# Two weight loads in two parts each over both DMA queues, a memset for padding zeros, a one-element first activation, and a list of tasks written anew

## The chip, the cores and the metric

The kernel runs on one core of a Trainium2 chip. The metric is the device time of one execution in microseconds (us); a kernel's time is the median of its runs. Before the change it is 303.88 us (three runs, 302.52 to 304.61). The engines are PE (TensorE, the matrix products; PEld are its weight loads), DVE (VectorE), ACT (ScalarE), POOL (GpSimd) and SP (SyncE, which here only issues DMAs). SP and ACT each issue DMAs on a queue of their own.

## The reference

A transformer block on x [2048, 640] in bf16: attention with a memory, then a dense layer with silu, both behind a layer norm and with a residual.

```
h  = x + attn(layernorm(x))        # 32 heads of 20, 4 segments of 512 tokens
    q, k, v = x @ wq, x @ wk, x @ wv
    per segment s:
        a_dot = softmax(q k^T / sqrt(20), causal) v
        a_mem = phi(q) M / (phi(q) z + 1e-6)
        o     = g * a_mem + (1 - g) * a_dot          # g = sigmoid(beta)
        M, z += phi(k)^T v, sum(phi(k))              # phi(t) = t + 1 or exp(t)
    attn = o @ wo
h2 = h + silu(layernorm(h) @ w1) @ w2                # 640 -> 1728 -> 640
```

## The kernel before

The work is cut into tasks (a load, a normalization of 128 tokens, a projection of one group of heads, a tile of scores, its exponentials, and so on), each with what it reads and writes. A list written out by hand, `ORDER`, gives the order in which the tasks are put on the engines; `/A`, `/D`, `/G`, `/S` after a name choose ACT, DVE, POOL or SP where a task can run on several, and numbers after a colon choose the buffers (PSUM banks, for instance). Each engine runs its own instructions strictly in the order of the list, and a tracker puts in the semaphore waits. So what stands before a task on its engine, and what it waits for, is all that sets its time.

Each of the four segments (512 tokens) goes through: layer norm and transposition of x (`n1_st` statistics, `n1_r` one over the root, `n1_ap` normalizing; then for segment 0 `n1_tp`, five products with the identity on PE, and `n1_te`, the copy of the transposed block to SBUF, and for the others a DMA transpose `n1_tr`); projections `pr` to q and k with their evacuation `qe`; values `v` with their evacuation `ve`; scores `qk` with their exponentials `e` on ACT, masks `mk` on POOL; products with the values `av`, evacuation `oe`, transposition back `tn` and normalizing `nm`; the memory `kt`, `mz`, `ma`, `mb`; the output projection `wo`; layer norm 2 (`n2_`); and the dense layer `h1`, `th`, `s`, `h2`, `o`, `out`. In segment 0 the tokens are taken in halves, x (the first 256) and y (the others). In a name like `pr020x` the digits are segment, group of heads, and 0 for q or 1 for k; in `e0x0` the group comes first.

The front, which the change touches most:

- SP and ACT issue the loads (lines 576 and 579): SP block 0 of x (`x0`), wq, three fifths of wv, blocks 4 to 7 of x, wo, beta, and then the parts of w1 and w2's last rows; ACT block 1 (`x1`), blocks 2 and 3 (`x2`), wk, the rest of wv.
- wq and wk come in the layout of the reference, 20 columns a head, and are rearranged for tiles of 32 rows a head: for each of five groups of heads a task `re_wq0` to `re_wq4` and `re_wk0` to `re_wk4`, of two or three copies each, on DVE (line 693) or ACT (line 691). Every one of them waits for the whole weight.
- `zpad` (line 592, DVE) zeroes a small tile. `warm` (line 594, ACT) is the first activation: it takes tanh of those zeros into the two last rows of w2's tile (128x1280), which the loads `w_w2_4` and `w_w2_5` then fill in part. The table of functions is loaded just ahead of it.
- `fill29` and `fill15` are products with zeros (line 613, 44 of them, 128x256) that feed nothing: PE runs them while it has no data.
- Block 1's and block 2's statistics run on ACT (lines 733 and 736), block 0's and block 3's on DVE (lines 741 and 744).
- `pr` products are at line 855, their evacuations at 863 (ACT) and 864 (DVE); scores at 932, their exponentials at 943.

## Time and profile before

| | us |
|---|---|
| median of three runs | 303.88 |
| the profiled execution | 303.13 |
| its span | 301.4 |
| first products with wq start | 10.43 |
| first scores start | 15.47 |
| first exponential starts | 15.86 |
| first evacuation of values starts | 27.40 |
| last product ends, about | 299.1 |

The span is the time from the first to the last instruction of one execution; some time lies around it. A row of the profile gives the start and the length of a group of instructions of one form; in brackets stand the idle time of the engine before it and what ended that. The rows of the stretches give how long each engine was busy in that stretch, the number of its instructions, the clock that PE was granted as a share of full speed, and the load of the DMA engines.

### The profile page before, as it was taken

To read this page: it belongs to the slowest core of one execution; us is meant where nothing else is said; L and a number is where in the kernel's file an instruction comes from. 1 tells how busy PE (TensorE), PEld (TensorE's weight loads), DVE (VectorE), ACT (ScalarE), POOL (GpSimd) and SP (SyncE) were. 2 spreads that over 40 slices of the span, in tenths; PEclk is the share of its full clock that TensorE was granted. 3 is DMA by queue.
4 is the path that set the end of the run, shared out by engine and by line. 5 is a ranking of instruction groups with operands and counts; after the bars stand their busy time and mean duration, and the time that the engine had idled before them with its cause. 6 is when DMAs were issued, how large, how long until landed. Compare 5 with 4: busy or idle time off the path is not lost.

```text
span 301.4 us, 7509 instructions
## 1 busy us (share of the span) xinstructions
PE 289.2 (96%) x2995; PEld 172.9 (57%) x3017; DVE 222.7 (74%) x516; ACT 226.0 (75%) x322; POOL 141.0 (47%) x267
## 2 busy tenths in 40 slices
PE   8799789999999999999999999999999999999996
PEld 6576445455655655656644544466565457764575
DVE  3879977977649789989679885868956786844613
ACT  6799998999999999999589889986778841004500
POOL 6678933344627555745647247574763430200000
PEclk9799999999999999999999999999999999999999
DMA  7998524405454301261741300234220013321001
GB/s 254 362 370 125 96 56 118 107 17 157 79 108 90 59 19 21 40 97 22 110 126 42 81 4 20 39 70 73 66 65 24 0 24 65 67 65 46 0 30 59
DMA packets 48723, 24.66 MB, mean 82 GB/s; under 512 B 39153, under 2 KB 47601, under 8 KB 48689
## 3 DMA queue, kind: packets, MB, share of 16 engines
q1 hardware_dynamic: 45116, 19.92, 29.4%
q10 hardware_dynamic: 3572, 4.27, 4.9%
q8 instruction: 24, 0.39, 0.5%
q14 instruction: 11, 0.08, 0.1%
HBM read 10.41 MB, written 2.62 MB: 43 GB/s over the span
## 4 chain that ended last, share of the span: by engine, by line
PE 68%; DVE 15%; ACT 10%; POOL 3%; issue 2%; ACTq 1%; DVEq 0%; POOLq 0%
PE ps_all L1235 18%; PE ps_all L1193 15%; PE ps_all L855 9%; ACT PT L943 7%; PE ps_all L1158 6%; PE ps_all L932 5%; PE ps_all L820 5%; PE ps_all L975 4%; DVE stt L741 3%; PE ps_all L1004 2%; PE ps_all L1008 1%; POOL PT L954 1%; DVE oTs L990 1%; PE ps_all L1097 1%; DVE on L1041 1%
## 5 line engine op out<-in xcount | busy, mean ns | idle before, releaser
L943 ACT ACTIVATE PT<-ps_all 128x1024 bf16<-128x1024 f32 (+1 forms) x168 | 156.6, 988 | 16.8 <-PE ps_all L932 16.1
L954 POOL TENSOR_SCALAR_AFFINE_SELECT PT<-PT 128x512 bf16<-128x512 bf16 x128 | 82.1, 645 | 68.7 <-ACT PT L943 66.1
L1235 PE MATMUL ps_all<-w_sb,sT 128*128 128x320 bf16 (+2 forms) x462 | 64.8, 295 | 0.1
L1193 PE MATMUL ps_all<-hT,w_sb 128*128 128x512 bf16 (+1 forms) x315 | 60.4, 335 | 1.1 <-issue 0.6
L1202 ACT ACTIVATE th<-ps_all 128x512 f32<-128x512 f32 (+2 forms) x70 | 34.7, 510 | 34.4 <-PE ps_all L1193 26.9
L1235 PEld LDWEIGHTS ps_all<-w_sb,sT 128*128 128x128 bf16 x462 | 43.2, 98 | 18.6 <-issue 2.4
L1208 DVE SCALAR_TENSOR_TENSOR sT<-th,ps_all 128x512 bf16<-128x512 f32 (+2 forms) x70 | 38.0, 558 | 12.7 <-ACT th L1202 11.9
L1193 PEld LDWEIGHTS ps_all<-hT,w_sb 128*128 128x128 bf16 x325 | 30.0, 98 | 24.0 <-issue 2.3
L1248 DVE SCALAR_TENSOR_TENSOR x_tok<-ps_all,x_tok 128x640 bf16<-128x640 f32 (+3 forms) x18 | 13.4, 748 | 22.3 <-PE ps_all L1235 22.1
L762 POOL TENSOR_TENSOR rst<-rst,eps_c 128x1 f32<-128x1 f32 x32 | 18.3, 574 | 23.3 <-DVE rst L756 21.2
L741 DVE BATCH_NORM_STATS2 stt<-x_tok 128x6 f32<-128x320 bf16 x60 | 26.3, 479 | 2.1 <-DMA x_tok<-in_A_x_dram 1.7
L1049 POOL TENSOR_TENSOR otok<-on 128x320 bf16<-128x320 bf16 x24 | 19.4, 811 | 14.7 <-DVE on L1041 14.7
L1158 PE MATMUL ps_all<-wo_sb,oT 128*128 128x320 bf16 x160 | 24.3, 299 | 0.5 <-DVE Vx L831 0.5
L975 PE MATMUL ps_all<-PT,Vx 128*32 128x256 bf16 (+3 forms) x576 | 23.1, 287 | 1.1 <-DVE rd L1021 0.7
L864 DVE CAST QK<-ps_all 128x512 bf16<-128x512 f32 x24 | 16.4, 684 | 5.4 <-PE ps_all L855 5.2
L1041 DVE TENSOR_TENSOR on<-ps_all,rd 128x640 bf16<-128x640 f32 x24 | 19.8, 824 | 0.8
L1158 PEld LDWEIGHTS ps_all<-wo_sb,oT 128*128 128x128 bf16 x160 | 14.8, 98 | 8.0 <-issue 2.7
L990 DVE TENSOR_SCALAR oTs<-ps_all,lsc 128x256 bf16<-128x256 f32 (+1 forms) x30 | 17.8, 610 | 1.3 <-PE ps_all L975 1.0
L820 PE MATMUL ps_all<-wv_sb,xT 128*128 128x320 bf16 x120 | 18.3, 299 | 0.4 <-DVE otok L1023 0.3
L975 PEld LDWEIGHTS ps_all<-PT,Vx 128*32 128x32 bf16 x576 | 12.2, 96 | 11.0 <-issue 3.2
L768 DVE TENSOR_SCALAR xn_rot<-x_tok,mvt,rst 128x640 bf16<-128x640 bf16 x32 | 14.8, 468 | 4.8 <-POOL rst L762 4.8
L855 PE MATMUL ps_all<-xT,wkr 128*128 128x512 bf16 x70 | 17.6, 380 | 0.5 <-issue 0.3
(88 smaller groups left out, 353.6 us busy)
## 6 DMA issues: line engine op xcount, KB each, us to landing
w_sb<-in_B_w_dram SPq DMA_DIRECT2D x5, 432.0 KB, 11.9
x_tok<-in_A_x_dram SPq DMA_DIRECT2D x3, 640.0 KB, 11.2
out_dram<-x_tok SPq DMA_DIRECT2D x9, 160.0 KB, 1.8
w_sb<-in_B_w_dram SPq DMA_DIRECT2D x2, 480.0 KB, 4.3
out_dram<-x_tok ACTq DMA_DIRECT2D x6, 160.0 KB, 2.0
sT<-in_A_wq_dram SPq DMA_DIRECT2D x1, 800.0 KB, 6.5
sT<-in_A_wk_dram ACTq DMA_DIRECT2D x1, 800.0 KB, 10.2
wo_sb<-in_A_wo_dram SPq DMA_DIRECT2D x1, 800.0 KB, 13.2
```

The costliest lines, as they stand in the source:

```text
L741: T.add(DV, lambda e, hh=hh: e.bn_stats(out=stt[:, s, 6 * hh:6 * hh + 6], in_=xb[:, 320 * hh:320 * hh + 320]), reads=R((xa, xsub)), writes ...
L820: fns.append(lambda e, c=c, hh=hh: e.matmul(bank(ps, hh)[:, 0:320], lhsT=xT_[:, c, 128 * i:128 * i + 128], rhs=wv_sb[:, c, 320 * hh:320 * ...
L855: fns = [lambda e, kc=kc: e.matmul(bank(ps)[:, lo:hi], lhsT=wt[:, kc, c, :], rhs=xT_[:, kc, lo:hi], start=(kc == 0), stop=(kc == NC - 1)) ...
L943: T.add(AC, lambda e: e.activation(out=pt[:, pta.slot, q0:q0 + 2, 0:width], in_=sc3[:, b0:b0 + 2, 0:width], func=ACT.Exp, scale=SCALE), re ...
L954: T.add(PO, lambda e: e.affine_select(out=v, in_=v, pattern=[[0, 4], [1, 128]], compare_op=ALU.is_ge, fill=0.0, base=0, channel_multiplier ...
L975: fns.append(lambda e, j=j, r=r, h=h, pa=pa, pt=pt, co=co, q0=q0, ji=ji: e.matmul(bank(po)[32 * r:32 * r + 32, q0:hi], lhsT=Vx[:, vx.slot, ...
L1041: T.add(DV, lambda e: e.tensor_tensor(out=on[:, ona.slot, :, :].rearrange("p b (x e) -> p b x e", e=DH), in0=v[:, :, :, 0:DH], in1=r2.unsq ...
L1158: fns.append(lambda e, c=c, hh=hh: e.matmul(bank(ps, hh)[:, 0:320], lhsT=oT[:, c, 128 * i:128 * i + 128], rhs=wo_sb[:, c, 320 * hh:320 * h ...
L1193: fns = [lambda e, c=c: e.matmul(bank(ps)[:, lo:hi], lhsT=w1_sb[:, c, 128 * f:128 * f + 128], rhs=hT[:, c, lo:hi], start=(c == 0), stop=(c ...
L1202: T.add(AC, lambda e: e.activation(out=th[:, tha.slot, lo:hi], in_=bank(ps)[:, lo:hi], func=ACT.Tanh, scale=0.5), reads=R((ps, [0])), writ ...
L1208: T.add(DV, lambda e: e.scalar_tensor_tensor(out=sT[:, f, lo:hi], in0=th[:, tha.slot, lo:hi], scalar=1.0, in1=bank(ps)[:, lo:hi], op0=ALU. ...
L1235: fns.append(lambda e, f=f, t0=t0, fr=fr, hh=hh, n=n: e.matmul(bank(pa, hh)[:, 0:n], lhsT=sT[:, f, t0:t0 + 128], rhs=w2_sb[:, fr, c0 + 320 ...
```

## The change

- wq and wk are each loaded in two parts, rows 0 to 383 on SP's queue and rows 384 to 639 on ACT's. The rearranging tasks wait for both parts.
- w2's padding zeros come from a memset (`w2z`, DVE), and `warm` writes a single element per partition to a tile of its own, `wj`.
- The list is written anew, with other engines for some tasks: in the front, ACT takes one block's statistics (block 0) instead of two, and three rearranging tasks (`re_wq1`, `re_wq4`, `re_wk0`) instead of one (`re_wq4`); there are 38 fillers in three tasks instead of 44 in two. Later, ACT takes `oe1x` and `ma00`; `ve21` goes to DVE; of the loads of w2's main parts, `w_w2_0` and `w_w2_1` go from ACT's queue to SP's and `w_w2_2` from SP's to ACT's; `vt16` (a copy of the heads that lie across tiles) goes from ACT's queue to SP's. PE's products keep nearly their order; at the end the last outputs are ordered otherwise.

```diff
@@ ORDER (first rows, and single rows of the rest)
-x1:3 mt0:0 epsc halfc mta0 mt1 epsg0 mt2 iota mta1 mtb1 x0:7 w_q:0 mm5 x2:5,0 w_k w_wv0:0 x4:1,2,4,6 w_wo:0 beta mta2
-mtb2 mt3 mta3 w_wv1 zpad sel warm:0 w_w2_4 w_w1_2:0 x8/S:8,9,10,11 w_w1_1 n1_st0/D:1,0 mm10 n1_st1/A:6 w_w1_0 w_w1_4
-n1_r0/G n1_ap0:0 mtb0 w_w2_5 mm6 mtb3 n1_r1/D n1_st3/D:0 w_w1_3 n1_r3/G n1_st2/A:2 n1_ap1:1 re_wq0/D:0 re_wq1/D
-n1_r2/G n1_ap3:2 mm11 re_wq2/D mm8 n1_ap2:3 re_wq3/D mm1 mm7 mm4 mm0 re_wk0/D:0 re_wk1/D fill29:0 fill15:1 re_wk2/D
-re_wk3/D n1_st6:5 n1_tp0:3 n1_te0/A:0 vpad1 mm9 vpad0 mm3 n1_tp1:0 n1_r6/G n1_te1/A mm2 re_wq4/A pr020x:2 n1_tp2:3
-n1_te2/A qe020x/A:0 pr000x:0 n1_tp3:6 n1_te3/A pr010x:1 qe010x/A:0 qe000x/A:0 pr001x:3 qe001x/A pr011x:4 qe011x/A
-qk0x0:0 e0x2:0 pr001y:5 e0x0 pr021x:6 qe001y/D qe021x/A n1_st4:7 n1_r4/G pha001:2 re_wk4/D pr040y:7 qe040y/A:0 ex001:1
+x1:3 mt1:0 mt0 halfc x0:7 w_q1:0 x2:5,0 mta0 mtb0 mm2 mm9 w_q0 w_k0 mt3 w_wv0:0 x4:1,2,4,6 iota w_wo:0 beta w2z/D:0
+zpad w_w2_4 w_w1_2:0 w_w1_4 w_w2_5 epsc sel mta3 vpad1 w_k1 w_wv1 x8/S:8,9,10,11 warm n1_st0/A:1,0 vpad0 mtb3 mm8
+n1_st1/D:6 n1_r1/D n1_ap1:1 mta1 w_w1_1 re_wq1/A:0 re_wq0/D n1_r0/G n1_ap0:0 re_wq2/D epsg0 n1_st3/D:0 mtb1 mm3 mt2
+mta2 mm11 mm1 n1_r3/G mtb2 n1_st2/D:2 n1_r2/D n1_ap3:2 re_wk1/D:0 n1_ap2:3 w_w1_0 w_w1_3 re_wk4/D re_wk3/D re_wq3/D
+fill6:0 fill27:1 fill5:2 mm7 mm6 mm4 mm5 mm10 mm0 n1_tp1:0 n1_te1/A:0 re_wk2/D n1_tp0:4 n1_te0/A pr020x:7 pr000x:2
+pr010x:0 re_wq4/A n1_tp3:3 re_wk0/A pr001x:5 qe000x/A:0 qe010x/A:0 qe020x/A:0 n1_te3/A qe001x/A n1_tp2:0 n1_te2/A
+pr011x:2 qk0x0:3 pr040y:7 pr001y:0 qe011x/D e0x0:0 e0x2 mk0x_0 qe001y/D qe040y/A:0 qk1x0:1 e1x0:1 pha001:2 mk0x_256
...
-nm4x:0 pha011:2 av1x:7 mk0yb_256 e7x2:2 oe1x/D:0 e7x0 mk7x_0 ve02/A phb011 n1_r8/G n1_ap8:3 qk5x0:0 v11:4 mk7x_256
+qk6x0:1 mk5x_256 oe1x/A:0 e6x2:1 e6x0 mk6x_0 mk6x_256 pha011:2 phb011 tn2x:7 av7x:0 nm2x:1 mk0yb_256 oe7x/D:1 tn1x:7
...
-ma13 oe11/A:0 ve20/D:0 n2_ap2:2 n2_tr2 e12e0:0 e12e2 mk12e_0 mk13a_0 mk12e_256 phb111 v21:0 ve21/A mz12:7 ma12 mz10:2
+e13b0:1 ma10 e13b2 mk12e_0 mk13b_0 mk13b_384 ve21/D mk12e_256 pr210:2 qe210/D:0 ex210:0 pr231:3 qk14a0:4 qe231/D:0
...
-o15_1 out15_1/A h2_13_0:4 h2_12_0:0 h2_12_1 h2_12_2 h2_12_3 o12 out12/S h2_15_1_0 h2_13_1 h2_13_2 h2_13_3 o13 out13/A
-h2_15_2_0 h2_15_3_0 o15_0 h2_15_0_2:6 h2_15_1_2 out15_0/A h2_15_2_2 h2_15_3_2 o15_2 out15_2/S
+h2_12_2 h2_12_3 o12 out12/S h2_15_2_0 h2_15_3_0 o15_0 out15_0/S h2_15_2_2 h2_15_3_2 o15_2 out15_2/A
@@ build
+    wj = sb("wj", [128, 1], F32)
...
-    load_w("q", wraw[:, 0, :, :], cw(A_wq), -99, 6.58, [(sT0, ["q"])], "fix", (SP,))
-    load_w("k", wraw[:, 1, :, :], cw(A_wk), -99, 8.51, [(sT0, ["k"])], "fix", (AC,))
+    for wi, (k, A_w) in enumerate((("q", A_wq), ("k", A_wk))):
+        load_w(k + "0", wraw[:, wi, 0:3, :], cw(A_w[0:384, :]), -99, 4.0, [(sT0, [k + "0"])], "fix", (SP,))
+        load_w(k + "1", wraw[:, wi, 3:5, :], cw(A_w[384:640, :]), -99, 2.7, [(sT0, [k + "1"])], "fix", (AC,))
...
-    G.task("warm", {AC: 1.15}, lambda e_: T.add(AC, lambda e: e.activation(
-        out=w2_sb[:, NF - 1:NF + 1, :], in_=zpad[:, 0:1].unsqueeze(2).to_broadcast([128, 2, D]), func=ACT.Tanh),
-        reads=R((C, ["zpad"])), writes=R((W["w2"], [4, 5]))), [(C, ["zpad"])], [(W["w2"], [4, 5])], -100)
+    G.task("warm", {AC: 0.2}, lambda e_: T.add(AC, lambda e: e.activation(
+        out=wj[:, :], in_=zpad[:, 0:1], func=ACT.Tanh), reads=R((C, ["zpad"])), writes=R((C, ["wj"]))),
+        [(C, ["zpad"])], [(C, ["wj"])], -100)
+    G.task("w2z", {PO: 1.3, DV: 0.4}, lambda eng: T.add(eng, lambda e: e.memset(w2_sb[:, NF - 1:NF + 1, :], 0.0),
+           writes=R((W["w2"], [4, 5]))), [], [(W["w2"], [4, 5])], -100)
...
-            rr, ww = [(sT0, ["qk"[wi]])], [(W[k], [c])]
+            rr, ww = [(sT0, ["qk"[wi] + "0", "qk"[wi] + "1"])], [(W[k], [c])]
```

The numbers in a task's declaration (4.0, 1.3, 0.4 and the like) are a planner's costs; they change nothing in the instructions.

More of the change, by code (lines that the diff above doesn't have):

```diff
@@ new lines @@
+nm1x:3 av3x:4 oe3x/D:0 ve11/A:1 qk0ya0:0 e0ya2:5 tn7x:7 nm7x:2 tn3x:4 nm3x:1 mz00:5 ma00/A:0 mb00:0 av5x:6 oe5x/D:0
+av6x:7 e0ya0 oe6x/D:1 qk1ya0:2 e1ya2:0 tn5x:6 nm5x:3 tn6x:7 nm6x:0 ot1:0 ot0 v10:0 ve10/D kt01:1 e1ya0 qk2ya0:4
+e2ya0:2 av0y:2 v12:0 oe0y/D:1 e2ya2 qk2yb0:2 w_w2_0/S e2yb0:1 e2yb2 mk2yb_0 mk2yb_256 ve12/D wo1:6 rs1 qk3ya0:0 wo0:4
+n2_st1:5 tn0y:7 nm0y:1 rs0 n2_r1/G n2_ap1:3 e3ya0:3 e3ya2 n2_st0:3 n2_r0/D n2_ap0:1 av1y:6 oe1y/A:0 qk4ya0:0 e4ya2:4
+pr101:7 v13:5 ve13/D e4ya0 qk3yb0:0 n2_tr1:0 qe101/A:0 pha101:2 n2_tr0 e3yb0:5 e3yb2 mk3yb_0 pr120:4 av2y:7 ex101:2
@@ new lines @@
+e16e0:5 e16e2 mk16e_0 pr230:4 qe230/D vt211/S vt27/S pha230:0 mk16e_256 vt22/S v22:6 vt25/S vt24/S ve22/D pha240:0
+pha231:0 phb231 ex220:0 qk17b0:2 ex240:2 phb240 vt28/S e17b0:3 vt21/A vt210/S h1_0_13_1:0 th0_13_1:1 s0_13_1 e17b2
+mk17b_0 h1_0_11_1:1 wo6:6 rs6 th0_11_1:0 ex230:1 qk18b0:2 e18b0:0 s0_11_1 mk17b_384 e18b2 mk18b_0 av16:0 oe16/D:1
+wo7:6 phb230 rs7 n2_st7:4 n2_r7/G qk17a0:0 e17a2:6 mk18b_384 e17a0 mk17a_0 wo4:4 rs4 n2_st6:6 ex241:2 h1_0_3_1:7
+th0_3_1:0 n2_r6/G h1_0_9_1:6 th0_9_1:1 qk18e0:0 wo5:4 e18e0:1 e18e2 s0_3_1 s0_9_1 n2_ap7:0 rs5 n2_ap6:2 mk18e_0
```

173 lines of the change are left out of this document (82 added, 91 removed).

## The prediction, made before the changed kernel was run

> **What bounds the kernel now.** I read the page first, then busy time in stretches, then the engines' timelines of the first 28 us, then the DMA issues.
>
> ```profile
> span 301.4 us, 7509 instructions
> ...
> PE 289.2 (96%) x2995; PEld 172.9 (57%) x3017; DVE 222.7 (74%) x516; ACT 226.0 (75%) x322; POOL 141.0 (47%) x267
> ```
>
> PE is busy for all but 12.2 us. By stretches (time, PE, PEld, DVE, ACT, POOL, then the granted clock):
>
> ```profile
> 0.00:10.00 10.00, 7.12 (x54) 5.58 (x54) 4.60 (x17) 7.00 (x13) 6.53 (x30) 1.00 0.84 281
> 10.00:20.00 10.00, 9.57 (x87) 7.60 (x88) 7.88 (x31) 7.87 (x20) 5.89 (x22) 0.83 1.06 365
> 20.00:30.00 10.00, 9.86 (x103) 6.88 (x101) 9.83 (x34) 9.93 (x19) 9.10 (x23) 1.00 0.90 192
> 30.00:40.00 10.00, 8.08 (x143) 4.40 (x140) 9.63 (x30) 9.12 (x14) 9.19 (x17) 1.00 0.41 74
> 60.00:80.00 20.00, 19.30 (x249) 11.91 (x248) 15.39 (x42) 19.87 (x32) 8.86 (x15) 1.00 0.36 91
> ```
>
> From 20 us on nothing waits long for anything: PE, DVE and ACT are full together, and later PE and ACT. So time won at the front is kept only if all three get it. The front is the one stretch with slack, and it runs like this (start, length, engine):
>
> ```profile
> 1.11 6.38 PE L613 MATMUL ps_all<-zpad 128*128 128x256 bf16 x44 [1.11 <-DVE zpad L592]
> ...
> 2.92 1.28 ACT L594 ACT_TABLE_LOAD   x1 [2.92 <-issue]
> ...
> 4.21 1.27 ACT L594 ACTIVATE w_sb<-zpad 128x1280 bf16<-128x1280 bf16 x1
> ...
> 10.43 0.85 PE L855 MATMUL ps_all<-hT,wqr 128*128 128x256 bf16 x5 [1.23 <-DVE wqr L693]
> ...
> 11.96 2.46 DVE L693 COPY wkr<-sT 128x400 bf16<-128x400 bf16 x9 [0.44 <-DMA sT<-in_A_wk_dram]
> ...
> 15.47 0.34 PE L932 MATMUL ps_all<-w_sb 20*128 20x256 bf16 x8
> ```
>
> The first products start at 10.43, the rearranging of wk waits for its load at 11.96, the first scores (qk0x) start at 15.47, their exponentials (e0x) at 15.86. The loads (KB, us from issue to landing):
>
> ```profile
> sT<-in_A_wq_dram SPq DMA_DIRECT2D x1, 800.0 KB, 6.5
> sT<-in_A_wk_dram ACTq DMA_DIRECT2D x1, 800.0 KB, 10.2
> ...
> x_tok<-in_A_x_dram ACTq DMA_DIRECT2D x1, 320.0 KB, 5.4
> ```
>
> **The loads.** With their issue times 1.25, 1.73 and 1.23 (and 2.33 with 11.4 to landing for wv's second part) the queues deliver: SP 160 KB (block 0 of x) by 3.79, 960 KB (and wq) by 7.75, 1440 KB (and half of wv) by 10.52, 2080 KB by 13.58; ACT 160 KB by 3.98, 480 KB by 6.63, 1280 KB (and wk) by 11.93, 1600 KB by 13.73. I interpolate on these. After the change SP carries x0 160, wq 480, wk 480; ACT x1 160, wq 320, x2-3 320, wk 320. The wq parts end at 640 KB on SP, 6.17, and 480 KB on ACT, 6.63: wq is there 1.1 us earlier. x2-3 end at 800 KB on ACT: 8.75 instead of 6.63, 2.1 later. The wk parts end at 1120 KB on both: 8.67 and 10.87, so wk is 1.1 earlier. wv's second part lands near 12.8, far ahead of its use at 25.7; x4 to x7 are some 0.7 later, behind 160 KB more.
>
> Equal shares of the two queues, half each of what both have brought by then (1609 KB at 7.75, 324 KB a us after it), would put x2-3 at 7.7 and wk at 9.7. But at 11.93 ACT's queue has brought 1280 KB and SP's some 1735, so I stay with the rows. The rule of equal turns is that of the Trainium skill, DMA: Bandwidth & Descriptors (Queues, rings and completion order: each DMA engine goes round robin over the queues by packets).
>
> **ACT's first work.** One more issue (0.57, as wk's row) puts the 1.28 table load at 3.49 to 4.77. The 1.27 activation shrinks to about 0.2 (the 128x32 exp takes 0.22): done at 4.99 instead of 5.48. ACT then does one block's statistics, 1.77 as in 5.39 to 7.16: 6.76. The second block that it had goes to DVE.
>
> **The zeros.** A DVE memset 128x640 in 32-bit words, ahead of zpad's. zpad's 128 took 0.17, so between 0.17 and five times that, 0.83; I take 0.7. It delays the fillers from 1.11 to 1.8, which PE has to spare: block 1 of x lands at 3.98, and statistics (1.10), rstd (0.15 and 0.56) and the normalizing (0.45) with hops of about 0.1 bring it to PE at 6.4. By the instruction order all 38 fillers (44 before) stand in one run ahead of the first transpose: none comes between products. Five products of the same 256 columns start to start take 1.07 at the half clock and 0.54 at the full, so 0.213 and 0.109 each; 44 in 6.38 us then turn fast at 4.0 (an estimate), and 38 from 1.8 end at 7.0, before ACT is free for the first copy of hT (7.6). If that cover is gone it costs up to 0.6.
>
> **The front, step by step.** POOL and DVE need 0.81 from the end of ACT's statistics to block 0's rstd (7.16 to 7.97) and 0.12 and 0.45 to apply it: 8.15. Transposes on PE 0.45, copy on ACT 0.70: 9.35. With 0.1 more the first products start at 9.45, 1.0 earlier; three of them at 0.54 end at 11.05. DVE meanwhile: wq's piece 8.55, x2-3 landed 8.75, two statistics of 0.89+0.21 to 10.95, rstd 0.15, apply 11.55, a piece of wk 11.9, apply 12.35. PE's transposes of blocks 3 and 2 follow at 11.6 and 12.55. ACT, in its order: wq's last piece 0.92 to 10.3; a piece of wk, waiting for 10.87, to 11.65; three evacuations (0.94) to 12.6; block 3's hT 13.25; the k evacuation 13.6, which opens the first scores at 13.65, 1.8 earlier; block 2's hT; e0x at 14.3, 1.55 earlier. ACT is the last to arrive.
>
> **The clock.** PE fell to half in the front:
>
> ```profile
> 10.00:11.00 1.00, 0.57 (x5) 0.93 1.07 362
> 11.00:12.00 1.00, 1.00 (x9) 0.50 1.07 364
> ```
>
> It lasts to 14.2, and products in it take 1.07 instead of 0.54. From 7.5 to 10.9 PE was busy for 1.19 of 3.4 us; after the change it has about 2.0, so I take full clock. With the fall it costs: the scores come at 14.6, e0x at 14.75, a loss of 0.45 of the gain. TensorE: Matmul & The Clock Gate in the Trainium skill (Part 1) has the clock drop after an idle window of about 3.4 us; the window here wasn't idle, so the trace shows the drop at a 35% busy share, and its bound remains open.
>
> **Up to 45 us.** ACT took 11.54 from e0x0 (15.86) to the first value evacuation (27.40) almost without a gap. The new list puts one more projection evacuation there (0.30): 26.15, a gain of 1.25. DVE ends its weight pieces at 14.25, about as before (14.34), but four pieces rather than one have come forward, with re_wk4's 0.50 done, and it hands oe1x (0.48) to ACT: 1.1 gained by 40 us. PE's 1.8 covers both. I take 1.2. ACT gets oe1x (0.47) and ma00 (about 0.3), which lie in its 0.88 of waits for PE at 36 to 39 us; without that cover they cost 0.77.
>
> **After 45 us.** The list shifts PE's work by few places. Off ACT go one of two w2 issues (0.38), a virtual-head issue (0.7) and ve21 (0.71): 1.8 us where ACT is over 94% full. The gain lies between nothing (DVE pays 0.83 for ve21; PE's idle is the ceiling, and from 60 to 140 it is 2.1 in all) and 1.8; I take 0.4, as most of PE's idle time is also in DVE's hands. The first w2 load now goes over SP's queue ahead of the two hT transposes; issued at 45.7 with 4.0 to landing it is done at 49.7, before the first of them at 50.7. Moving wk's and wq's issues on SP delays wo and beta by one issue, 0.5: both are used much later. At the tail the last product group is the same 128 columns, and o12 (0.82) now stands right before the last two outputs on DVE: -0.1.
>
> **Sum.** 1.2 + 0.4 - 0.1 = 1.5. The profiled execution took 303.13 (span 301.4 and 1.73 around it), so 301.6; it lies 0.75 under the median of the runs, 303.88, from which I get 302.4. One per cent, 3.0 us, is about what a measurement can tell.
>
> **Rivals.**
> - *More is kept* (300.6). If the queues do share equally, wk at 9.7 lets ACT go on at 10.3, and e0x comes at 13.7: 0.55 more. With ACT's relief worth 1.8 instead of 0.4, the gain is 3.3. For it: ACT at 19.87 of 20. Against: the shares above.
> - *Nothing arrives* (303.9). x2-3 are 2.1 later, and DVE, which now does both blocks' statistics, starts them then. If they land at 10 rather than 8.75, block 2's hT and DVE's remaining pieces slip by 1.25, and the 1.2 is gone.
> - *ACT becomes the bound of the first segment* (304.5, slower). If wk lands at 11.93 as before, e0x comes at 15.35 and ACT's lead of 0.5, less 0.3 for the extra evacuation, is 0.2; oe1x and ma00 then find no waits of ACT to hide in, 0.77, and the tail takes 0.1: 0.65 slower. It decides from about 11.4 on. For it: ACT is 9.93 of 10 busy there. Against: its waits at 36 to 39.
> - *It doesn't do what it says*: that holds for the fillers, which aren't between products. If the clock falls in spite of the earlier products, 0.45 is lost: 302.8, inside the forecast.
>
> **How the numbers follow.** Forecast 302.4: 0.52, own range 301.4 to 303.3. More kept: 0.16. Nothing: 0.15. ACT bound: 0.17. The range 300.6 to 304.6 takes in the three rivals at their prices and leaves out their far halves, 0.2 in all. Faster by over 1% (under 300.84): most of the second case, 0.14. Slower by over 1% (over 306.9) needs more than the third case prices, a stage of the redone list that fits worse on the chip: 0.06. Within: 0.80.
>
> **What would show it.** Right: wq's first piece before 7.2, first products near 9.5, first scores near 13.7, e0x near 14.3, the first value evacuation near 26.1, and ACT's share above 60 us a little lower. Wrong: wk's first piece later than 11.4; a granted clock of 0.5 after 9.5; DVE waiting for x2-3 beyond 9.5; or a front that is earlier and a stretch from 30 to 60 us with more PE idle time than its 2.65 us.

## The result and the profile after

The changed kernel takes 305.06 us (median of 20 runs, 303.47 to 306.57) and the kernel before, beside it, 303.38 (20 runs, 302.50 to 306.16). The ratio is 1.0042, with a 95% interval of 1.0023 to 1.0062: 1.3 us slower, where the prediction had 1.5 us faster. The profiled execution took 305.88, 0.8 more than the median; its span is 304.1.

The page of the profile after; before, the span was 301.4 us and PE was busy for 289.2:

```profile
span 304.1 us, 7512 instructions
...
PE 289.5 (95%) x2989; PEld 171.4 (56%) x3011; DVE 222.4 (73%) x506; ACT 225.4 (74%) x326; POOL 141.8 (47%) x273
```

The rows of the engines for the front of the changed kernel (start, length, engine; in brackets the idle time before and what ended it):

```profile
9.36 1.81 PE L859 MATMUL ps_all<-hT,wqr 128*128 128x256 bf16 x15 [0.80 <-ACT hT L790]
...
10.78 0.83 ACT L695 ACTIVATE wkr<-sT 128x400 bf16<-128x400 bf16 x2 [0.67 <-DMA sT<-in_A_wk_dram]
...
13.47 0.34 PE L936 MATMUL ps_all<-w_sb 20*128 20x256 bf16 x8
...
25.92 0.74 ACT L834 ACTIVATE Vx<-ps_all 128x640 bf16<-128x640 f32 x1
```

The first products (10.43 before) start 1.1 earlier, the first scores (15.47) 2.0 earlier, and the first evacuation of values (27.40) 1.5 earlier. The front did what it was meant to. By stretches (time, PE, PEld, DVE, ACT, POOL, granted clock, load of the DMA engines, GB/s) the changed kernel then shows:

```profile
20.00:30.00 10.00, 9.25 (x101) 5.68 (x99) 9.79 (x31) 9.18 (x18) 9.34 (x28) 1.00 0.87 194
30.00:40.00 10.00, 7.71 (x101) 4.03 (x101) 7.57 (x23) 7.25 (x12) 6.09 (x11) 0.83 0.34 72
60.00:80.00 20.00, 19.50 (x245) 11.24 (x246) 15.29 (x42) 19.86 (x31) 7.99 (x13) 1.00 0.39 99
120.00:140.00 20.00, 18.66 (x220) 11.42 (x219) 18.17 (x41) 17.82 (x27) 10.80 (x17) 1.00 0.32 62
```

Two stretches are new. Between 30 and 40 all three full engines have gaps (DVE 7.57 against 9.63, ACT 7.25 against 9.12), and the clock is 0.83. Between 120 and 140 PE is busy for 18.66 instead of 19.26, as the kernel before has it:

```profile
120.00:140.00 20.00, 19.26 (x226) 11.78 (x224) 18.64 (x42) 18.96 (x31) 13.04 (x23) 1.00 0.40 63
```

Here is the first of the two in the changed kernel, in PE's rows:

```profile
30.44 0.25 PE L1012 MATMUL ps_all<-ident,oTs 128*128 128x84 bf16 x2
32.10 0.51 PE L936 MATMUL ps_all<-w_sb 20*128 20x256 bf16 x8 [1.41 <-DVE rd L1025]
32.54 2.82 PE L824 MATMUL ps_all<-wv_sb,hT 128*128 128x320 bf16 x10
```

The row at 32.10 is `qk7x0`, the first scores of heads that lie across tiles. Their queries and keys come by twelve small copies `vt0…`, issued on SP's and ACT's queues. The bracket names a DVE instruction; the weight load of the same line shows what came last. From the waits of PE's weight loads (in all, times, longest), and SP's queue:

```profile
PEld ps_all L936 <- DMA w_sb<-w_sb: 1.5, 1, 1.5
```

```profile
22.00 7.42 SPq L899 DMA_DIRECT2D w_sb<-w_sb  x8
```

SP issues its eight copies in one unbroken run from 22.00 to 29.42. Before, the run was from 23.16 to 29.52:

```profile
23.16 6.36 SPq L895 DMA_DIRECT2D w_sb<-w_sb  x8
```

The last copy lands at 32.01 in this trace and at 32.27 in that of before, where `qk7x0` started at 32.33: there too it started as the last copy had landed, only that PE was busy until then. So the copies land 0.3 earlier, and `qk7x0` starts at 32.10, though the scores ahead of it are 1.3 to 3.1 earlier. While PE waits, its clock falls to half, and the ten products `v02` behind it take 2.82 instead of 1.5. The lead is gone and 0.9 us are lost when this execution comes to `qk2yb0` at 46 us. From there to the end of the products its lag grows from 0.9 to 2.6 us.

### The profile page after: what moved, and what is told of

Read it like the earlier page. It is cut to its first block, busy times and chain, and to the rows that moved or that the text cites. A ratio compares the mean times of both kernels' runs of the same rounds, so it can differ in the third digit from the quotient of the medians.

```text
span 304.1 us, 7512 instructions
## 1 busy us (share of the span) xinstructions
PE 289.5 (95%) x2989; PEld 171.4 (56%) x3011; DVE 222.4 (73%) x506; ACT 225.4 (74%) x326; POOL 141.8 (47%) x273
## 4 chain that ended last, share of the span: by engine, by line
PE 73%; DVE 11%; ACT 9%; DMA 3%; issue 2%; ACTq 1%; DVEq 0%
PE ps_all L1239 20%; PE ps_all L1197 16%; PE ps_all L859 9%; PE ps_all L824 7%; PE ps_all L936 6%; PE ps_all L1162 6%; ACT PT L947 6%; PE ps_all L979 4%; DMA sT<-in_A_wk_dram 3%; PE ps_all L1008 2%; PE ps_all L1101 2%; PE ps_all L1012 1%; DVE on L1045 1%; DVE sT L1212 1%; DVE x_tok L1170 1%
## 5 line engine op out<-in xcount | busy, mean ns | idle before, releaser
L1206 ACT ACTIVATE th<-ps_all 128x512 f32<-128x512 f32 (+2 forms) x70 | 34.6, 510 | 34.2 <-PE ps_all L1191 19.6
L745 DVE BATCH_NORM_STATS2 stt<-x_tok 128x6 f32<-128x320 bf16 x62 | 27.0, 477 | 0.8 <-DMA x_tok<-in_A_x_dram 0.5
L772 DVE TENSOR_SCALAR xn_rot<-x_tok,mvt,rst 128x640 bf16<-128x640 bf16 x32 | 15.7, 495 | 6.6 <-POOL rst L766 5.9
L979 PEld LDWEIGHTS ps_all<-PT,Vx 128*32 128x32 bf16 x576 | 12.2, 96 | 10.9 <-issue 4.1
L859 PE MATMUL ps_all<-xT,wqr 128*128 128x512 bf16 x68 | 17.2, 380 | 1.2 <-DVE x_tok L1170 0.7
```

The lines of the kernel that those rows point to most:

```text
L745: T.add(DV, lambda e, hh=hh: e.bn_stats(out=stt[:, s, 6 * hh:6 * hh + 6], in_=xb[:, 320 * hh:320 * hh + 320]), reads=R((xa, xsub)), writes ...
L859: fns = [lambda e, kc=kc: e.matmul(bank(ps)[:, lo:hi], lhsT=wt[:, kc, c, :], rhs=xT_[:, kc, lo:hi], start=(kc == 0), stop=(kc == NC - 1)) ...
L979: fns.append(lambda e, j=j, r=r, h=h, pa=pa, pt=pt, co=co, q0=q0, ji=ji: e.matmul(bank(po)[32 * r:32 * r + 32, q0:hi], lhsT=Vx[:, vx.slot, ...
L1206: T.add(AC, lambda e: e.activation(out=th[:, tha.slot, lo:hi], in_=bank(ps)[:, lo:hi], func=ACT.Tanh, scale=0.5), reads=R((ps, [0])), writ ...
```

## The experiments

The ratios are to the kernel before, run beside each kernel; a thousandth is 0.3 us. A difference between two kernels of the table, taken from their ratios, is uncertain by 0.8 to 1.1 us either way; a smaller one is not told from none. A lag below is the start of the same products against the profile of before.

| kernel | median, us | ratio (95%) |
|---|---|---|
| changed | 305.06 | 1.0042 (1.0023 to 1.0062) |
| v02_first | 305.38 | 1.0065 (1.0041 to 1.0088) |
| fill_ahead | 304.72 | 1.0037 (1.0020 to 1.0053) |
| heads_early | 307.26 | 1.0125 (1.0087 to 1.0162) |
| heads_first | 304.93 | 1.0036 (1.0015 to 1.0057) |
| no_head_wait | 304.78 | 1.0025 (1.0001 to 1.0050) |
| front_only | 304.23 | 1.0030 (1.0011 to 1.0050) |
| front_to_45 | 303.48 | 0.9992 (0.9966 to 1.0017) |
| fill_to_45 | 302.91 | 0.9980 (0.9958 to 1.0002) |
| fill8_to_45 | 302.82 | 0.9973 (0.9948 to 0.9999) |
| ya_ahead | 307.66 | 1.0137 (1.0103 to 1.0170) |
| rest_only | 306.20 | 1.0104 (1.0068 to 1.0141) |
| mid_before | 306.07 | 1.0085 (1.0055 to 1.0114) |
| phi_later | 307.86 | 1.0132 (1.0104 to 1.0161) |
| small_masks | 303.92 | 0.9996 (0.9964 to 1.0027) |
| ve21_on_act | 305.03 | 1.0036 (1.0010 to 1.0062) |
| split_only | 304.72 | 1.0046 (1.0027 to 1.0065) |
| no_split | 306.42 | 1.0075 (1.0048 to 1.0103) |
| memset_only | 303.28 | 0.9979 (0.9954 to 1.0003) |

**The wait at 32 us: other work into it, zeros into it, or the wait taken away.**

```diff
@@ v02_first
-... n1_tr7 qk7x0:1 e7x0:2 v02:5 n1_r8/D ...
+... n1_tr7 v02:5 qk7x0:1 e7x0:2 n1_r8/D ...
@@ fill_ahead
+... n1_tr7 fill11:5 qk7x0:1 e7x0:2 v02:5 ...
@@ no_head_wait (scores)
+            alt = 5 if name in ("5x", "6x", "7x") else 0
-                        _, qa, ka = operands(g)
+                        _, qa, ka = operands(g - alt)
```

> The changed kernel with one task moved: the ten value products v02 stand ahead of the scores qk7x0 on TensorE instead of behind them. Theory A (the copies for the virtual heads set qk7x0, TensorE idles 1.41 us there and the clock falls): qk7x0 still starts at 32.0 to 32.2, v02 takes 1.5 us in 30.7 to 32.2 at full clock, no half clock between 30 and 36, the products tn4x start near 33.0 instead of 34.9; of these 1.9 us at least half reaches the end, so 303.2 to 304.2 against 305.06 for the changed kernel and 303.38 for the kernel before. Theory B (the redone rest of the list is what costs, and the stretch around 32 us is covered by ACT and DVE): tn4x earlier too, but the end stays at 304.8 to 305.3.

> The changed kernel with eleven products of zeros (1.2 us at full clock, a free bank) ahead of qk7x0, so that TensorE is busy while it waits but gets nothing done. Theory A: the wait stays, qk7x0 at 32.0 to 32.3, but the clock stays full and v02 takes 1.5 instead of 2.82: tn4x near 33.7 instead of 34.9, the end 0.4 to 1.2 below the changed kernel, 303.9 to 304.7. If the half clock is not caused by the idle stretch: half clock again at about 32, and the time is that of the changed kernel or 0.1 more. Theory B: clock full, end unchanged at 304.8 to 305.3.

> The changed kernel, but the first scores of the heads that lie across tiles (qk5x, qk6x, qk7x, segment 0, first half) read the queries and keys of groups 0 to 2 instead of the copied ones, so nothing on TensorE waits for the copies there; the copies are still issued, the amount of work is the same, and these scores are of other heads. Theory A (the landing of the copies alone holds qk7x0): qk7x0 starts at 31.0 to 31.4 instead of 32.07, when e1yb has emptied its banks, no half clock, qk2ya0 at 42.0 to 42.9 instead of 43.8, end 303.6 to 304.5 against 305.06. Rival (banks or ACT's exponentials hold it): qk7x0 at 31.8 or later, end 304.8 to 305.3.

In no_head_wait `qk5x0` to `qk7x0` are scores of other heads, so its output is another; the scores in that place and the values behind them run so:

```profile
30.92 0.35 PE L937 MATMUL ps_all<-w_sb 20*128 20x256 bf16 x8 [0.33 <-DVE oTs L995]
31.20 1.53 PE L824 MATMUL ps_all<-wv_sb,hT 128*128 128x320 bf16 x10
```

1.18 us earlier than in the changed kernel, at full clock: the copies hold `qk7x0`, and with the idle stretch the fall of the clock is gone from this profile. But the end missed the expected 303.6 to 304.5, and falls by only 0.5 us by the ratios, which is not told from none. The lead of 1.4 at 35 us is 0.3 at 45: PE waits some 0.8 for DVE and 1.1 us for a mask on POOL at 37 us:

```profile
37.26 0.35 PE L980 MATMUL ps_all<-PT,Vx 128*32 128x256 bf16 x8 [1.07 <-POOL PT L959]
```

That wait leads back to the same queue. SP issues two transpositions behind its copies, from 30.19; DVE waits 0.88 us for one of them at 34.2 (`n1_ap7`), POOL 2.48 us for what DVE does behind it (`n1_r8`), and only then come POOL's masks. So the copies are the first, not the only, thing behind SP's run that holds PE. With fill_ahead the clock stays full and `v02` takes 1.53; the lag at 45 us is 0.0 instead of 0.9, though this execution's first scores come 0.6 later. By the ratios the zeros are worth 0.15 us here and 0.6 in the old order (fill8_to_45 against front_to_45, below), neither told from none and both less than the 1.3 that `v02` lost: the clock does not fall in every execution (in ve21_on_act's profile it did not, behind a wait of 0.85 for the copies). In v02_first the wait only moved:

```profile
31.32 1.52 PE L824 MATMUL ps_all<-wv_sb,hT 128*128 128x320 bf16 x10
32.90 0.35 PE L936 MATMUL ps_all<-w_sb 20*128 20x256 bf16 x8
...
34.93 0.34 PE L936 MATMUL ps_all<-w_sb 20*128 20x256 bf16 x8 [1.50 <-ACT PT L947]
```

PE fills its gap with `v02`, but the exponentials of `qk7x0` start as late as before, and the next scores wait 1.50 for the banks that they empty. The profile gained 0.6 at the end, the median is not better: 305.38, where 303.2 to 304.2 was expected.

**The copies sooner: by the queues, or by the chain ahead of them.**

```diff
@@ heads_early
-... n1_ap5:3 n1_tr5:0 ...
-... vt00/S vt06/S v00:4 ... vt09/A v01:6 n1_r9/D vt010/S e0yb0 vt03/A ve01/A ...
+... vt04/A vt010/A ... vt00/S vt06/S vt03/S n1_tr5:0 v00:4 ... vt09/A ...
@@ heads_first (up to 45 us; behind it the order of before)
-... qe000y/A qk4x0:2 e4x2:5 pr021y:1 vt04/A pr020y:6 qe021y/A pha021:2 e4x0 mk4x_0 qe020y/A ...
+... qe000y/A pr021y:1 pr020y:6 qe021y/A qe020y/A qk4x0:2 e4x2:5 vt05/A pha021:2 e4x0 vt04/A ...
```

> The changed kernel with SP's queue relieved ahead of qk7x0: the transpose n1_tr5 is issued behind the virtual-head copies instead of ahead of them, the copy vt010 goes from SP's to ACT's queue and vt03 from ACT's to SP's. Theory A: the last copy is issued by 28.3 instead of 29.4 and lands near 30.5 instead of 32.0; qk7x0 starts near 31.0 (then the exponentials e1y bound it), no half clock near 32, tn4x 2 us earlier than in the changed kernel; end 302.9 to 304.2. Rival (qk7x0 waits for the bank or the exponentials, not for the copies): qk7x0 stays at 32.0 and the end at 304.8 to 305.3. Theory B: qk7x0 earlier, the end unchanged.

> The changed kernel up to 45 us, then the order of the kernel before, and ahead of 32 us the chain to qk7x0 put first: the projections pr021y and pr020y stand ahead of the scores qk4x0 and their evacuations on ACT ahead of the exponentials e4x, the copy vt010 goes to ACT's queue, and ACT issues its five copies each behind a long activation. Theory (the serial issue of the copies on SP's queue, and the evacuations of groups 0 to 2 ahead of it, set qk7x0): SP's last copy is issued by 28.7 at the latest instead of 29.4, qk7x0 starts at 31.0 to 31.6, at 45 us 0.4 to 0.9 ahead of the kernel before, end 302.4 to 303.2. Rival (the copies land late whatever their issue, by the DMA engines' load from the transposes): qk7x0 at 32.0 or later, end 303.2 to 304.5.

Both missed. In heads_early ACT's issue of `vt010` took 1.42 us instead of 0.7 and pushed the evacuations back; SP's last copy was issued at 29.88, `qk7x0` started at 32.09, and DVE then waited 0.9 us for the transposition that was put back; with a clock at half from 39.7 to 46.5 the lag grew to 2.9 us by 45 us. In heads_first SP was done at 27.69, but ACT, which issued five copies, one of them 1.54 long, became the last: its exponentials came late, and `qk7x0` started at 33.03, waiting for them:

```profile
33.03 0.35 PE L936 MATMUL ps_all<-w_sb 20*128 20x256 bf16 x8 [0.57 <-ACT PT L947]
```

Its clock was at half from 41.0 to 44.4, which adds to its time. So in 20 to 30 us SP's queue and ACT are both full, and an issue that leaves the one is paid on the other. Nor does the issue settle it alone: over all profiles of this front the last issue ends between 28.2 and 30.4 and the last copy lands 2.1 to 3.3 us after that. In ve21_on_act SP was done at 28.23, 1.3 before its time in the kernel before, and the last copy still landed at 31.83, 0.4 before. What holds the copies after the issue was not tested by itself.

**Front and rest taken apart.** Lists joined where both have done the same tasks.

```diff
@@ front_only:  list of the change up to qk7x0 | list of before
@@ rest_only:   kernel before up to qk7x0      | list of the change
@@ front_to_45: list of the change up to qk2yb0 (45 us) | list of before
@@ fill_to_45:  the same with fill11:5 ahead of qk7x0
@@ fill8_to_45: the same with fill8:5
@@ ya_ahead:    front_only with qk0ya0 e0ya2 e0ya0 and v02 ahead of qk7x0
```

> The changed kernel up to the scores qk7x0 (list, loads, zeros, first activation), and from there the list of the kernel before (with the banks of tn0x and qk7x0 renamed). Theory A: wait and half clock as in the changed kernel, tn4x about 1 us later than in the kernel before, and that lag stays to the end: 304.0 to 304.7. Theory B (the rest of the redone list costs): the stretch at 32 us recovers, end at 303.4 or below, faster than the changed kernel by 1.7 or more.

> The kernel before up to the scores qk7x0 (its loads, its first activation, its list), and from there the list of the changed kernel. Theory (two losses that add: front with wait and half clock, and the redone rest): the stretch at 32 us as in the kernel before, then the rest alone loses 0.4 us near 97 us (TensorE waits for an addition on DVE ahead of pr220) and 1.0 to 1.4 us between 115 and 130 (scores wait for DVE): 1.2 to 1.9 slower than the kernel before at the end, 304.5 to 305.2 against 303.4. Rival (the rest loses only because the front reaches it shifted): within 0.4 of the kernel before.

> The combination of the front of the changed kernel and the rest of the kernel before, with the scores qk0ya0 and their exponentials, and the values v02, put ahead of qk7x0, so that TensorE and ACT have work while the copies for the virtual heads are on their way. Theory A (the copies' issues on SP's and ACT's queues bound qk7x0, and nothing else does): no half clock, e7x starts at 32.9 to 33.6 directly behind e0ya, tn4x later in place but the products from qk1ya0 on 0.5 to 1.3 us earlier than in the kernel before; end 302.2 to 303.0 against 303.4. Rival (DVE or the buffers bound the stretch 30 to 45 us too): qk1ya0 at the time of the kernel before or later, end 303.2 to 304.2.

> The changed kernel with the eleven products of zeros ahead of qk7x0, up to the scores qk2yb0 (45 us), and from there the order of the kernel before (in one place n1_ap8 and n1_ap9 are exchanged, as the two lists had them). Theory of two losses: at 45 us level with the kernel before (within 0.4), no loss behind it, so 303.0 to 303.8: the whole gain of the front is swallowed by the wait for the virtual-head copies, and the list behind 45 us costs the rest. Rival (the redone list costs little, the medians differ for another reason): 304.4 to 305.0, like fill_ahead.

> The changed kernel up to the scores qk2yb0 (45 us), without products of zeros, and from there the order of the kernel before: the clean form of front_only, in its own banks. Theory: qk7x0 waits for the copies as in the changed kernel and the clock falls in some of the executions; profile at 45 us between 0.3 ahead of the kernel before and 1.2 behind, end 303.0 to 303.8, ratio 0.998 to 1.002, 0.1 to 0.6 above fill_to_45; the changed kernel's other 1.3 us are the redone list behind 45 us. Rival (without the fillers the front is a loss of its own): 304.2 or more.

> The same with eight products of zeros (0.9 us) ahead of qk7x0 instead of eleven, so that they end before the copies land in most executions: the candidate for a kernel that beats both. Theory: clock full throughout, 302.5 to 303.2, ratio 0.996 to 0.999. Rival (the 302.91 of fill_to_45 was chance): 303.3 to 303.8.

front_to_45 gives the split of the result: the front with the wait is 0.2 us better than before (0.9992, not to be told from none), the redone list behind 45 us costs the other 1.5 (1.0042 less 0.9992, uncertain by 1.0). The profiles agree: behind `qk8a0` at 69 us front_to_45 keeps its lag within 0.03 up to 136 us, where the changed kernel's grows from 1.0 to 2.2. (At 136.5 it waits 0.33 for a transposition, `oT<-otok`, which the list of before has as well, and it is 0.5 behind from there on.) front_only had a fault of its own: `tn0x` was put on bank 6, which `v02` also needs (it takes banks 5 and 6), so it tells less than front_to_45. In rest_only part of the loss (0.95 at 45 us) comes from the join: DVE waits 2.33 us at 37 us for a transposition that the old front issues later; its list behind that loses the same 1.7 as the changed kernel's. It missed its range, 304.5 to 305.2; the clock also fell in 6 of its 7 executions. ya_ahead missed for the same bank: `v02` waited 1.14 for it, the next scores 1.16 for ACT, and the clock fell for 10 us; whether exponentials ahead of `qk7x0` would help stays open.

With the filler and the order of before behind 45 us the ratios are 0.6 and 0.8 us better than before, the interval of fill8_to_45 just below 1. That is not the earlier front arriving. Each execution has a granted clock, and one window of 3.41 us at half the clock makes its mean 0.994 instead of 1.00 (half of 3.41 in some 301). The kernel before has such falls too, in 69 of the 125 executions that ran beside these kernels (in its profile the fall stands at 10.9 to 14.3 us). Sorted by it (us):

| kernel | executions without a fall | their median | median with one fall |
|---|---|---|---|
| before | 56 of 125 | 302.9 | 304.0 |
| changed | 14 of 20 | 304.7 | 305.7 |
| fill_ahead | 12 of 12 | 304.7 | |
| no_head_wait | 9 of 12 | 304.7 | 306.0 |
| front_to_45 | 7 of 12 | 303.2 | 304.0 |
| fill_to_45 | 11 of 12 | 302.9 | 305.9 (one) |
| fill8_to_45 | 12 of 12 | 302.8 | |
| small_masks | 8 of 12 | 303.4 | 305.4 |
| memset_only | 10 of 12 | 303.2 | 304.8 |

Among executions without a fall the new front with the order of before is at 302.8 to 303.2 and the kernel before at 302.9: the earlier front is worth nothing that can be told. The zeros gain the falls that stay away, 1.1 us each in the kernel before. The redone list costs about the same either way: 304.7 against 303.2, and 305.7 against 304.0.

**The list behind 45 us.** In the changed kernel PE waits 0.75 us at 97 for DVE's `rs2`, 0.39 at 122 and 0.76 at 130 for evacuations on DVE:

```profile
122.41 0.40 PE L936 MATMUL ps_all<-QK 20*128 20x384 bf16 x8 [0.39 <-DVE on L1045]
...
129.73 0.40 PE L936 MATMUL ps_all<-QK 20*128 20x256 bf16 x8 [0.76 <-DVE on L1045]
```

DVE's rows for the phi operations (128x512, SBUF to SBUF) there:

```profile
119.20 1.15 DVE L881 TENSOR_SCALAR phiK<-QK 128x512 bf16<-128x512 bf16 x2
124.94 0.91 DVE L887 TENSOR_TENSOR phiK<-phiK,ex 128x512 bf16<-128x512 bf16 x1
126.43 0.76 DVE L881 TENSOR_SCALAR phiQ<-QK 128x512 bf16<-128x512 bf16 x1
127.22 0.42 DVE L887 TENSOR_TENSOR phiQ<-phiQ,ex 128x512 bf16<-128x512 bf16 x1
127.56 0.76 DVE L887 TENSOR_TENSOR phiK<-phiK,ex 128x512 bf16<-128x512 bf16 x1
129.59 0.28 DVE L881 TENSOR_SCALAR phiQ<-QK 128x512 bf16<-128x512 bf16 x1
```

The same operation takes 0.28 or 0.76 (L881), 0.42 or 0.91 (L887). The kernel before has four of them (`pha201`, `pha221`, `phb201`, `phb221`) at 0.28 to 0.43, where the changed one has 0.51, 0.72, 0.91 and 0.76:

```profile
115.85 0.28 DVE L877 TENSOR_SCALAR phiK<-QK 128x512 bf16<-128x512 bf16 x1
...
118.11 0.39 DVE L877 TENSOR_SCALAR phiK<-QK 128x512 bf16<-128x512 bf16 x1
...
123.09 0.42 DVE L883 TENSOR_TENSOR phiK<-phiK,ex 128x512 bf16<-128x512 bf16 x1
...
124.96 0.43 DVE L883 TENSOR_TENSOR phiK<-phiK,ex 128x512 bf16<-128x512 bf16 x1
```

The eight from `pha200` to `phb221`, in the changed list all ahead of the wait at 130 us, take 5.10 us together instead of 3.80. From 114 to 136 us all phi operations take 7.08 in both kernels (15 of them before, 14 after): the new list mostly changes which of them are long, and makes it the early ones. The long ones lie beside work on POOL, masks and an addition:

```profile
119.51 0.69 POOL L958 TENSOR_SCALAR_AFFINE_SELECT PT<-PT 128x512 bf16<-128x512 bf16 x1
...
124.77 0.79 POOL L1053 TENSOR_TENSOR otok<-on 128x320 bf16<-128x320 bf16 x1 [0.29 <-DVE on L1045]
125.52 1.53 POOL L958 TENSOR_SCALAR_AFFINE_SELECT PT<-PT 128x512 bf16<-128x512 bf16 x2
```

Four kernels ask what of this costs the time: the order of before in the stretch, the phi operations a few places later, nine masks cut to a sixteenth of their columns (so the scores are only partly masked), and `ve21` back on ACT.

```diff
@@ mid_before: tasks from kt11 to s0_0_1 (106 to 125 us) in the order of before
@@ phi_later
-o1 out1/S pha111:1 phb110 ad8:0 e12a0 n2_tr3 mk12a_0 wo2:0 rs2 av10:7 ...
+o1 out1/S ad8:0 e12a0 n2_tr3 mk12a_0 wo2:0 rs2 pha111:1 phb110 av10:7 ...
-... pha201:1 pha221:0 ... nm14:3,0 ... pha210:0 phb210 phb221 kt22:0 ... nm15:0,0 ...
+... nm14:3,0 pha201:1 pha221:0 ... nm15:0,0 pha210:0 phb210 phb221 kt22:0 ...
@@ small_masks
-                    v = pt[:, pta.slot, :, co:co + 128]
+                    n = 8 if name in ("14b", "14e", "15a", "15b", "16b") else 128
+                    v = pt[:, pta.slot, :, co:co + n]
@@ ve21_on_act
-... ve21/D ...
+... ve21/A ...
```

> The changed kernel with one stretch, from the scores qk14a0 to the statistics pass of qk16b0 (about 106 to 125 us), in the order of the kernel before (banks of qk14a0 and pr231 renamed); the tasks are the same and so are their engines but for vt20 and vt23's place. Theory (DVE's phi operations take 0.3 us alone and up to 1.0 beside masks on POOL, and the redone order puts more of them beside masks, ahead of the evacuations that the scores wait for): the eight phi operations of DVE between 114 and 130 us take about 3.2 to 3.9 us in all instead of 5.1, TensorE's 2.2 us of waits for DVE there shrink below 1.2, the end 0.7 to 1.3 below the changed kernel: 303.8 to 304.4 against 305.06. Rival (ve21's move to DVE at 105 us is what fills DVE): no gain, since ve21 stays where it is.

> The changed kernel with seven phi operations of DVE moved by a few places behind evacuations that TensorE waits for: pha111 and phb110 behind rs2, pha201 and pha221 behind nm14, pha210, phb210 and phb221 (and the transposition kt22 that reads it) behind nm15. Engines and all else unchanged. Theory (DVE's place in the redone order costs the 0.7, 0.39 and 0.76 us that TensorE waits at 97, 122 and 130 us): these three waits are together below 0.8 us, end 303.8 to 304.5 against 305.06. Rival (DVE is full there, so the same work comes due elsewhere): waits of the same sum at later places, end 304.8 to 305.4.

> The changed kernel with five pairs of masks on POOL (groups 14 to 16 of scores of segment 1, between 112 and 127 us) cut from 128 to 8 columns a head, so that they take about 0.1 us instead of 0.65; waits and order unchanged, these scores are only partly masked. Theory (DVE's phi operations are slowed from 0.28-0.43 to 0.5-1.0 us while POOL works, and DVE is full there): the phi operations that lay beside these masks take 0.3 to 0.45 us, TensorE's waits of 0.39 and 0.76 us for DVE shrink to below 0.4 together, end 304.0 to 304.6. Rival (DVE's order alone, POOL does not slow it): durations and waits as in the changed kernel, end 304.8 to 305.4.

> The changed kernel with ve21, one of the moves between engines in the redone list, back on ACT. Theory (DVE has 0.5 us of idle time right behind ve21 at 106 us, so its 0.82 there is paid by nobody, and the waits come from 112 us on): end within 0.3 of the changed kernel, 304.8 to 305.4. Rival (its 0.82 on DVE is what DVE lacks later): end 304.4 or below, the waits at 122 and 130 us shorter.

small_masks is the clear one. A mask took 0.26 instead of 0.67 (not the 0.1 that was expected), and the phi operations beside the cut masks went back to the short lengths; three, beside POOL's additions, stayed long (0.86, 0.90, and the first of the two at 120.90, 0.50):

```profile
117.72 0.86 DVE L881 TENSOR_SCALAR phiQ<-QK 128x512 bf16<-128x512 bf16 x1
118.61 0.43 DVE L887 TENSOR_TENSOR phiQ<-phiQ,ex 128x512 bf16<-128x512 bf16 x1
120.90 0.74 DVE L881 TENSOR_SCALAR phiK<-QK 128x512 bf16<-128x512 bf16 x2
126.22 0.90 DVE L887 TENSOR_TENSOR phiK<-phiK,ex 128x512 bf16<-128x512 bf16 x1
127.71 0.28 DVE L881 TENSOR_SCALAR phiQ<-QK 128x512 bf16<-128x512 bf16 x1
128.03 0.43 DVE L887 TENSOR_TENSOR phiQ<-phiQ,ex 128x512 bf16<-128x512 bf16 x1
128.37 0.42 DVE L887 TENSOR_TENSOR phiK<-phiK,ex 128x512 bf16<-128x512 bf16 x1
```

PE's waits at 122 and 130 are gone (one of 0.55 for DVE at 121 came in). From `qk15a0` to `qk17a0` (115 to 136 us) the lag grows by 0.11 instead of 1.07, and the kernel is 1.4 us faster than the changed one by the ratios, 1.3 by the executions without a fall of the clock. (The profiled execution is the slowest of its twelve, 306.34: a late front, the fall at 33 us, and 0.5 lost near 106 us, where PE waits 0.41 for a transposition. All that lies ahead of the cut masks.) Besides DVE's relief that holds what the cut masks give to the products that wait for them, so the gain bounds DVE's part from above. ve21_on_act changes nothing that can be told: 305.03, PE's waits of 0.39 and 0.76 as in the changed kernel. DVE has 0.5 us idle behind `ve21` there.

phi_later missed on the wrong side. Its waits at 122 and 130 for the evacuations went, but the work that was put back came due at the next place, and at a worse one, an evacuation that a product of values waits for:

```profile
133.24 1.53 PE L824 MATMUL ps_all<-wv_sb,xT 128*128 128x320 bf16 x10 [1.97 <-DVE QK L868]
```

DVE is nearly full there (18.17 of 20 us from 120 to 140); moving its work back by hand does not make less of it. mid_before is inconclusive as a whole: 2.3 us were lost at once, from 102 to 112 us, where PE waits 0.57 for a transposition and 0.86 for ACT's exponentials. But inside, where the order of before runs (`qk15a0` to `qk16a0`), its lag grows by 0.0, and the changed kernel's by 0.74, although its eight phi operations take 4.55 us and not the 3.2 to 3.9 that were expected.

**The other parts alone.**

```diff
@@ split_only (list of before): w_q, w_k -> w_q1 w_q0 w_k0 ... w_k1; rest as before
@@ no_split (list of the change): w_q1 w_q0 w_k0 ... w_k1 -> w_q ... w_k
@@ memset_only (list of before): + w2z/D:0 ahead of zpad; warm writes wj
```

> The kernel before with one part of the change alone: wq and wk in two parts over both queues, list and engines otherwise as before (w2's rows by the wide first activation). Theory A: wq's parts land about 1 us earlier, x's blocks 2 and 3 some 2 us later; first products 0.5 to 1.2 earlier, but ACT does the statistics of block 2 only then and qk0x0 is 0.3 earlier to 1.0 later than before (15.46); qk7x0 stays at 32.1 to 32.5, end within 0.5 of the kernel before. Rival (an earlier wq goes through to the end): end 0.8 or more below the kernel before.

> The changed kernel with one part undone: wq and wk are whole loads again, wq on SP's and wk on ACT's queue; memset, first activation and list as changed. Theory A (qk7x0 is set by the copies and the evacuations of groups 0 to 2 ahead of them): wq lands about 1.1 us later, the first scores 0.7 to 1.5 us later than in the changed kernel, qk7x0 at 32.0 to 33.0, end 304.8 to 306.0. Rival (the split is the harm, through the late blocks 2 and 3 of x): end 304.3 or below.

> The kernel before with only the second part of the change: the zeros of w2's padding by a memset on DVE ahead of zpad's, and the one-element first activation. Theory: ACT is free for its first statistics 1.0 us earlier, DVE's first memset delays the fillers by 0.6; but the first products still wait for wq's rearranging at 10.4, so first scores at 15.2 to 15.6 and the end within 0.4 of the kernel before. Rival (the front is bound by ACT's start): scores 0.8 or more earlier and the end 0.5 to 1.0 below the kernel before.

The split of the loads makes the kernel before 1.4 us slower and the changed kernel 1.0 us faster, the second at the edge of what can be told; theory A's end was missed in both, by 0.8 above its range in split_only and by 0.4 in no_split. In the old list ACT takes block 2's statistics, and block 2 lands later now; ACT waits for it, and the first scores come 0.6 later. The new list gives that block to DVE. The clock also fell in 11 of split_only's 12 executions, against 12 of 20 of the kernel before beside it. The memset with the short activation alone is 0.6 us better by the ratio, with an interval that reaches 1.0003. Its clock fell in 2 of 12 executions, that of the kernel before beside it in 20 of 35, and without a fall the two are at 303.2 and 303.5: most of the 0.6 is falls that stay away. The profiled execution, 304.71, is not a typical one (its fillers take 7.36 instead of 6.38 us, the first scores come 0.4 later, and PE waits 0.95 at 137.6 for a transposition).

## Why the prediction was wrong

**Loads, zeros, front, clock: right.** ACT starts wk's piece at 10.78 (10.87 predicted), the memset takes 0.59 (0.7), the fillers end at 7.41 (7.0), first products 9.36 (9.45), first scores 13.47 (13.65), `e0x` 13.87 (14.3), first evacuation of values 25.92 (26.15). The clock did not fall in the front of this execution. But its fall in the profile of before, 10.85 to 14.27, was taken for the kernel's own, and it is not in every execution: 69 of 125 of the kernel before have a fall, 6 of 20 of the changed one. The prediction priced it at 0.45; executions of the kernel before with one are 1.1 longer than those without. This execution was a good one: in the fifteen profiles of kernels with this front the first scores lie between 1.1 and 2.4 ahead of the profile of before, as wq's parts land up to 1.4 later (ACT's first piece at 6.47 here, 7.90 in v02_first).

**"Up to 45 us … I take 1.2": wrong by 1.0.** Measured is 0.2 (front_to_45), with the clock held 0.8 (fill8_to_45), and without falls of the clock on either side nothing that can be told. The step that failed is "PE's 1.8 covers both": it looked at ACT's and DVE's busy time between `e0x` and the values, and took PE as the follower. It did not follow the third input of PE's next scores, the virtual-head copies, nor the transpositions behind them on SP's queue. The row for that stood in the profile before: SP's eight issues at 23.16 to 29.52, in one run. That run followed a front that is 2.0 us earlier only in part: its first issue came 1.2 earlier (22.00), one issue of 1.79 ate that, and the copies landed 0.3 earlier. In the other profiles of this front they landed between 1.4 earlier and 0.8 later than before, so the long issue is not the whole of it. Nor are the copies all: with their wait taken away (no_head_wait) 0.3 is left at 45 us, and by the rows of that profile DVE and POOL then wait on SP's transpositions, which was not tested by itself. The prediction's own sign of failure, PE idle for more than 2.65 us from 30 to 60, came true with 3.0.

**"After 45 us … I take 0.4": wrong by 1.9, and wrong in its bounds.** Measured is a loss of 1.5, the tail included. The step counted work taken off ACT and bounded the gain "between nothing … and 1.8". That the end was not below nothing had no reason behind it but that few products move. DVE's price for the same order was not looked at: its phi operations cost two to three times as much beside POOL's work, and the new list puts the early ones there (5.10 us for eight instead of 3.80), ahead of evacuations that the scores wait for. small_masks shows this for the 1.07 us from 115 to 136; the 0.4 at 97 us (`rs2`, behind a `phb110` of 1.01) is the same by its rows but was not tested by itself. `ve21`, the largest item of that sum, is worth nothing that can be told.

On DVE and POOL the Trainium skill has a rule, SBUF — State Buffer (Who interferes with whom): the two share one pair of SBUF ports under a lock, and the loser is blocked rather than slowed. The trace agrees in that only operations beside POOL are long, up to 0.91 and 1.01 us, against at most 0.30 and 0.43 alone; the 0.91 at 124.94 ends 0.29 behind the POOL addition that ends at 125.56, which fits a block but does not show one. That rule, laid beside the two lists, speaks against the change, and would have put an end below nothing under the step.

**The rivals.** "More is kept" and "nothing arrives" named other causes (the shares of the queues, x2-3 late) and neither occurred. "ACT becomes the bound" had the sign and half the size (0.65), but not the mechanism: wk landed as forecast. The fall of the clock, priced at 0.45 at the front, came at 32 us instead. Two prices do not follow from their own terms: "more is kept" adds up to 1.2 + 0.55 + 1.8 - 0.1 = 3.45, not 3.3, and with "the 1.2 is gone" the other 0.3 still arrives, which is 303.6, not 303.9.

**The tail: right.** 0.1 lost was forecast. From the end of the last product to the end of the span it is 2.30 before and 2.44 after, 0.14 lost.

## What to carry to other kernels

When a front is made faster, follow each input of the first product behind it, the small copies and the queue that issues them too: the gain ends at the first one that is serial and already full, and the next may stand on the same queue. A list that is written for one set of arrival times fits only those, as the split loads show, 1.4 us worse in the old list and about 1.0 better in the new. A reordering can have a price below nothing, and on DVE it is read from what POOL does at the same time. Where the clock falls in some executions and not in others, one profile shows one kind: compare executions of the same granted clock before a gain is put down to the change.
